# Moving the pieces of weight joining inside a chunk, the order of early loads, and the place of four conversions, in a fused attention and two-layer feed-forward kernel

## The chip, the cores and the metric

One core of one Trainium2 chip runs the whole kernel. The metric is device time in microseconds (us), from three runs of the kernel, of which the median stands here. One more execution was taken under the hardware profiler; every duration below comes from that one.

## What is computed

The reference, cut down to what matters:

```python
# attention: q, k, v are (4, 8, 576, 64), float32
scores = scale * q @ k.T + bias[h]           # ALiBi bias, causal window of 128
attn = softmax(scores); out = attn @ v       # -> x, (2304, 512)
# first layer: w_in (512, 2048), w_out (2048, 512)
h = x @ w_in
P = a0 + a1*h + a2*h*h + a3*h*h*h
Q = 1 + |b0|*|h| + |b1|*h*h
x = (P / (Q + 1e-6)) @ w_out
# second layer, other weights of the same sizes
h = x @ w_in
out = where(h > 0, h, exp(min(h, 0)) - 1) @ w_out
```

The weights of both layers arrive as float64. [...]

## The kernel before, in words

**Attention.** 16 units (a batch entry and a pair of heads each), software pipelined: iteration `t` of the loop at line 684 runs the table `STEPS` (line 18), in which each step names how many iterations it lies ahead or behind. q, k and v of a unit come by transfers that SyncE (SP) issues, in program order, from one queue. `load(u + 3, "qk")` is called at step `zT` (line 643), `load(u + 2, "v")` at step `Y` (line 648). There are two v buffers, so v of unit u+2 can only be fetched after step `Y` of unit u. `load_some(2)` (line 686) fetches two float64 weight tiles of the first layer in each of the iterations 0 to 11.

**Conversion.** A weight tile of the first layer takes five instructions: `conv_scale` (ScalarE, line 130), `conv_shift` (VectorE, line 138), `conv_or` (VectorE, line 148), `conv_hi` (the rounded part, line 156 or 158) and `conv_lo` (the rest, line 162). `PLAN` (line 32) says how many tiles are converted beside which attention unit: 24 of the 32 there. Then `CONV_AFTER` (line 33) calls `conv_step` six times in the last iterations, and `conv_step` is called in the first layer's first block (line 1267). `conv_step` puts its VectorE parts into a list, `put_off`, which `go_on` works off one by one.

**First layer.** Tokens go in five blocks (512, 512, 512, 256, 512 columns), a block in 16 chunks of 128 hidden units; chunk number `s` runs over all 80 (line 1263). TensorE alternates `gemm1(s)` (12 matmuls, line 287) and `gemm2_T(s - 3)` (12 matmuls, line 725); each product is three passes, over high and low parts of both factors. Between them lies `rational` (line 302): ScalarE makes the square, |h|, two affine terms (lines 311 to 314), later a logarithm and an exponential (lines 325, 326), which give 1/Q; VectorE makes the rest (lines 319 to 340), and from chunk 5 on GpSimd (POOL) makes the low part of the result (line 337). `rational(s)` finishes chunk s-1 and begins chunk s on the same queues.

`rational` takes callables that are put between its instructions. In blocks 1 and 2 they **join** second-layer weights: per chunk two half tiles n and n+1, each `join_scale` (ScalarE, line 130, reads a fetched half, writes a buffer: `space_u` for even n, `space_w1` for odd n), `join_shift` (VectorE, line 138), `join_words` (VectorE, line 800), then a copy out to DRAM (line 810) and the fetch of half n+3 (line 776). There are 26 such chunks, 13 in each of the two blocks.

At a block's end `split_x` (line 256) splits the next block's input into high parts (ScalarE, line 268) and low parts (VectorE, line 269), four of each, into the buffers that `gemm1` has just read. `conv_until` in `gemm1` and `gemm2_T` would force a conversion that is late.

**Second layer.** Its order comes from a planner (`in_order`, line 1153). Neither the planner nor its costs are touched.

The scale in the middle of a joined chunk is placed by this call (lines 1280 to 1283):

```python
rational(
    s, after=lambda: join_scale(nj + 1),
    beside=(first_join, lambda: join_shift(nj + 1), lambda: join_end(nj + 1)),
)
```

Of the kernel before, what the change touches and what calls it, by code (L numbers as in the profile page):

```python
# [28 lines left out]
)  # L29


PLAN = (0, 0, 0) + (2,) * 12 + (0,) * 4
CONV_AFTER = ((15, "E8"), (15, "R1"), (14, "V1"), (15, "T01"), (15, "T11"), (15, "V1"))
AHEAD = {
    (14, "T00"): 1, (14, "T10"): 1, (14, "T11"): 2, (14, "V0"): 1, (14, "V1"): 2, (14, "Y"): 1,
# [9 lines left out]
def kernel(  # L45
# [125 lines left out]
    def go_on():  # L171
        if put_off:
            put_off.pop(0)()
# [79 lines left out]
    def bank(n, shape, name):  # L253
        return psum.tile(shape, F32, tag=f"b{n}", name=name)

    def split_x(j, rounds="AAAA"):
        t0, n = BL[j]
        if j == 0:
            for tag in ("qa", "qb", "ta", "bi"):
                cut(tag, SIZE[tag], F32R)  # L260
        parts = {"hi": [], "lo": []}
        for c in range(KD):
            src = xT[:, c, t0:t0 + n]
            hi, lo = row1(f"hi{c}", j * KF), row1(f"lo{c}", j * KF)
            if rounds[c] == "D":
                nc.vector.tensor_copy(hi, src)
            else:
                nc.scalar.activation(out=hi, in_=src, func=AF.Copy)  # L268
            nc.vector.tensor_tensor(out=lo, in0=src, in1=hi.bitcast(F32), op=ALU.subtract)  # L269
            parts["hi"].append(hi)  # L270
            parts["lo"].append(lo)
        return parts
# [26 lines left out]
        for c in range(4):  # L299
            yield from gemm1(c, c, x1[0], 4 + c)  # L300

    def rational(c, old=True, beside=3 * (lambda: None,), after=lambda: None):


        old = old and c - 1 in q_t
        new = c in h_t
        if new:
            h = h_t.pop(c)
            h2, ee, qq, rr = [row1(nm, c) for nm in ("h2", f"ee{c % 2}", f"qq{c % 2}", f"rr{c % 2}")]
            qa = bank(6, [P, width(c)], "qa") if c > 3 else qq  # L310
            nc.scalar.activation(out=h2, in_=h, func=AF.Square)  # L311
            nc.scalar.activation(out=qa, in_=h, func=AF.Abs, scale=b_abs[:, 0:1])  # L312
            nc.scalar.activation(out=ee, in_=h, func=AF.Identity, scale=a_sb[:, 1:2], bias=a_sb[:, 0:1])  # L313
            nc.scalar.activation(out=h, in_=h, func=AF.Identity, scale=a_sb[:, 3:4], bias=a_sb[:, 2:3])  # L314
        if old:
            qq0, ee0, rr0 = q_t.pop(c - 1)
            hi, low = row1(f"ghi{c % 3}", c - 1), row1(f"glo{c % 3}", c - 1)
            g_t[c - 1] = (hi, low)
            nc.vector.tensor_tensor(out=hi, in0=ee0, in1=rr0, op=ALU.mult)  # L319
        beside[0]()  # L320
        if new:
            nc.vector.scalar_tensor_tensor(  # L322
                out=qq, in0=h2, scalar=b_abs[:, 1:2], in1=qa, op0=ALU.mult, op1=ALU.add
            )
            nc.scalar.activation(out=rr, in_=qq, func=AF.Ln, bias=c_q)  # L325
            nc.scalar.activation(out=rr, in_=rr, func=AF.Exp, scale=-1.0)
            q_t[c] = (qq, ee, rr)
        after()
        beside[1]()
        if old:  # L330
            nc.vector.scalar_tensor_tensor(
                out=qq0, in0=qq0, scalar=EPSC, in1=hi.bitcast(F32), op0=ALU.add, op1=ALU.mult
            )
        beside[2]()
        if old:
            nc.vector.tensor_tensor(out=ee0, in0=ee0, in1=qq0, op=ALU.subtract)  # L336
            (nc.gpsimd if c > 4 else nc.vector).tensor_tensor(out=low, in0=ee0, in1=rr0, op=ALU.mult)  # L337
        if new:
            nc.vector.tensor_tensor(out=h, in0=h2, in1=h, op=ALU.mult)  # L339
            nc.vector.tensor_tensor(out=ee, in0=ee, in1=h, op=ALU.add)  # L340


    def attention():
        with ExitStack() as es:
# [284 lines left out]
            def run(step, u):  # L629
                if step[0] in CONV:  # L630
                    if 0 <= u < len(PLAN) and int(step[1]) < PLAN[u]:
                        n = sum(PLAN[:u]) + int(step[1])
                        eng = ENG.get(step)
                        CONV[step[0]](order[n], *([eng] if eng else []))
                        if step[0] == "s":
                            to_conv.pop(0)
                elif 0 <= u < NU:
                    RUN[step](u)
                    if u == 0 and step == "kT":
                        warm(1)  # L640
                    if step == "zT":
                        if u + 3 < NU:
                            load(u + 3, "qk")
                        elif u == NU - 1:
                            load_some(4)
                    elif step == "Y":
                        if u + 2 < NU:
                            load(u + 2, "v")
                        else:
                            load_some(2)  # L650

# [30 lines left out]

            first = -max(late for _, late in STEPS)
            for t in range(first, NU + 2):
                if 0 <= t < 12:
                    load_some(2)
                if t == NU - 1:
                    x1[0] = split_x(0, "DADA")
# [22 lines left out]
    def experts():  # L711
# [519 lines left out]
        def prepare(s):  # L1231
            f = s - LAST
            if f == 3:
                load_wi(0)
            if f == 14:
                load_wi(1)
                for e in raw_ones(0):
                    load_raw(0, e)

            def copies():  # L1240
                for fn in AT_ACT.get(f, []):
                    fn()

            def next_one():
                if f >= 3 and AT_DVE:
                    AT_DVE.pop(0)()
            rational(s, beside=(lambda: None, next_one, next_one), after=copies)

        def joins(s):

# [12 lines left out]
        for s in range(NCH):  # L1263
            o = s - SK
            j, f = divmod(s, KF)
            if j == 0 and f % 2 and f > 2:
                conv_step(to_conv, later=True)
            if s >= 4:
                run_all(gemm1(s, f, x1[j], (4, 5, 7)[(s - 4) % 3]))
            if f == KF - 1 and j + 1 < NB:  # L1270
                x1[j + 1] = split_x(j + 1)
            if o >= 0:
                gemm2_T(o)
            if joins(s) == 2:

                def first_join():
                    join_shift(nj)
                    join_end(nj)

                rational(  # L1280
                    s, after=lambda: join_scale(nj + 1),
                    beside=(first_join, lambda: join_shift(nj + 1), lambda: join_end(nj + 1)),
                )
            elif joins(s):
                rational(s, beside=(lambda: None, lambda: join_shift(nj), lambda: join_end(nj)))
            elif s >= LAST:
                prepare(s)
            else:
                rational(s, beside=(go_on, go_on, go_on))
            nj += joins(s)  # L1290
            if s == KF - 2:
                for n in range(3):
                    load_half(n)
            if joins(s + 1):
                join_scale(nj)
# [41 lines left out]
```

## Time and profile before

| what | value |
|---|---|
| median of 3 runs (lowest, highest) | 948.56 us (947.55, 950.12) |
| the profiled execution | 951.53 us, its span 949.7 us |
| mean granted TensorE clock, share of full speed | 0.992 |
| TensorE busy with matmuls | 920.9 us (97%) |
| VectorE busy | 787.3 us (83%) |
| ScalarE busy | 710.8 us (75%) |
| GpSimd busy | 175.9 us (19%) |

The profiled execution took 2.97 us longer than the median of the three runs; its span, first to last instruction, is 1.83 us shorter than its own time. A sum worked out on the span is a difference, and is taken off 951.53 us and off 948.56 us alike.

A row of the timeline reads: start in us from the span's beginning, duration, engine, line of the kernel, operation, what it writes and reads, and in brackets how long the engine sat idle before it and what ended that. A row's duration reaches from its start to its end; on one engine the next row may start before that end.

### The profile page before, as it was taken

What the parts mean: (1) busy time and instruction counts of PE and PEld (TensorE: products, weight loads), DVE (VectorE), ACT (ScalarE), POOL (GpSimd) and SP (SyncE); (2) the same over time, 40 slices, a digit from 0 to 9 for tenths busy, and PEclk for the clock granted to TensorE, in tenths of its full rate; (3) what the DMA queues carried; (4) which work ended last, traced back from release to release, by engine and by line L of the source; (5) the groups of instructions that cost most, each with busy time, mean ns of one, the idle gap of its engine ahead of it and who ended that gap; (6) DMA issues with size and microseconds to landing.
All of it is one profiled execution on the core that took longest, in us unless ns stands there. A gap on an engine that the chain in (4) does not pass through costs nothing.

```text
span 949.7 us, 15573 instructions
## 1 busy us (share of the span) xinstructions
PE 920.9 (97%) x5110; PEld 776.2 (82%) x5110; DVE 787.3 (83%) x1773; ACT 710.8 (75%) x1510; POOL 175.9 (19%) x238
## 2 busy tenths in 40 slices
PE   8999999999999899979999999999999999999998
PEld 5777777888877687759988888898989898989897
DVE  7699999998788877887889898999967778787653
ACT  6899997887767777778888777676867566766553
POOL 4466661122122211222222220000000000000000
PEclk9899999999999999999999999999999999999999
DMA  9899842000333323230010033445334332442201
GB/s 172 212 247 247 222 148 69 1 12 23 112 121 106 94 90 126 99 109 1 1 35 1 1 101 110 133 153 203 111 128 139 102 99 71 167 140 90 78 0 67
DMA packets 112560, 98.27 MB, mean 103 GB/s; under 512 B 62816, under 2 KB 86368, under 8 KB 112480
## 3 DMA queue, kind: packets, MB, share of 16 engines
q1 hardware_dynamic: 109936, 96.57, 34.5%
q10 hardware_dynamic: 2544, 0.72, 0.4%
q8 instruction: 40, 0.66, 0.3%
q14 instruction: 40, 0.33, 0.1%
HBM read 79.96 MB, written 17.30 MB: 102 GB/s over the span
## 4 chain that ended last, share of the span: by engine, by line
PE 70%; DVE 19%; DMA 4%; ACT 3%; issue 2%; DVEq 0%; SPq 0%; ACTq 0%
PE acc L951 21%; PE m L935 18%; PE acc L725 14%; PE h L287 13%; DVE space_g L319 2%; DVE xT L340 2%; DVE xT L336 2%; DVE h L339 2%; DVE pr_wi L518 1%; DMA joined_wi<-space_u 1%; DVE pr_wo L518 1%; DMA v<-in_v_dram 1%; DVE cvt L148 1%; DMA joined_wo<-space_u 1%; PE s_ps L492 1%
## 5 line engine op out<-in xcount | busy, mean ns | idle before, releaser
L725 PE MATMUL acc<-space_g,w_wo 128*128 128x512 f32 (+1 forms) x960 | 217.2, 372 | 9.1 <-POOL space_g L337 8.3
L725 PEld LDWEIGHTS acc<-space_g,w_wo 128*128 128x128 f32 x960 | 168.5, 190 | 46.0 <-POOL space_g L337 15.1
L337 POOL TENSOR_TENSOR space_g<-xT,space_r 128x512 fp32r<-128x512 f32 (+1 forms) x76 | 89.4, 1176 | 329.3 <-DVE xT L336 239.3
L951 PE MATMUL acc<-op_wo,space_g 128*128 128x512 f32 x432 | 108.2, 393 | 0.0
L287 PE MATMUL h<-space_qa,w_wi 128*128 128x512 f32 (+1 forms) x320 | 91.9, 371 | 4.1 <-ACT space_qa L268 3.4
L951 PEld LDWEIGHTS acc<-op_wo,space_g 128*128 128x128 f32 x432 | 80.5, 188 | 14.7
L311 ACT ACTIVATE space_u<-h 128x512 f32<-128x512 f32 (+1 forms) x80 | 44.3, 554 | 62.9 <-DVE h L339 43.3
L997 ACT ACTIVATE space_u<-space_r 128x384 f32<-128x384 f32 x48 | 25.1, 523 | 75.3 <-DVE space_r L991 74.4
L287 PE MATMUL h<-space_qb,w_wi 128*128 128x512 f32 (+1 forms) x240 | 76.1, 371 | 3.8 <-DVE space_qb L269 3.8
L935 PE MATMUL m<-xo_wi,op_wi 128*128 128x384 f32 x336 | 77.3, 337 | 0.0
L935 PE MATMUL m<-xo_wo,op_wi 128*128 128x384 f32 x336 | 76.4, 335 | 0.0
L287 PE MATMUL h<-space_ta,w_wi 128*128 128x512 f32 (+1 forms) x240 | 76.1, 372 | 0.0
L287 PEld LDWEIGHTS h<-space_qa,w_wi 128*128 128x128 f32 x320 | 57.5, 189 | 15.0 <-ACT space_qa L268 4.2
L322 DVE SCALAR_TENSOR_TENSOR xT<-space_u,b_abs,qa 128x512 f32<-128x512 f32 (+1 forms) x76 | 52.2, 687 | 16.6 <-ACT qa L312 16.4
L325 ACT ACTIVATE space_r<-xT,c_q 128x512 f32<-128x512 f32 (+1 forms) x80 | 55.1, 689 | 13.7 <-DVE xT L322 13.4
L935 PEld LDWEIGHTS m<-xo_wo,op_wi 128*128 128x128 f32 x336 | 60.9, 188 | 4.1
L935 PEld LDWEIGHTS m<-xo_wi,op_wi 128*128 128x128 f32 x336 | 60.6, 188 | 0.0
L287 PE MATMUL h<-space_bi,w_wi 128*128 128x512 f32 (+1 forms) x160 | 59.6, 372 | 0.0
L319 DVE TENSOR_TENSOR space_g<-xT,space_r 128x512 fp32r<-128x512 f32 (+1 forms) x80 | 51.4, 643 | 9.5 <-PE h L287 0.5
L313 ACT ACTIVATE xT<-h,a_sb 128x512 f32<-128x512 f32 (+1 forms) x80 | 59.3, 741 | 0.0
L1001 ACT ACTIVATE space_u<-space_u,c_m 128x384 f32<-128x384 f32 x96 | 57.5, 611 | 1.6
L314 ACT ACTIVATE h<-h,a_sb 128x512 f32<-128x512 f32 (+1 forms) x80 | 57.4, 717 | 0.0
(187 smaller groups left out, 2120.2 us busy)
## 6 DMA issues: line engine op xcount, KB each, us to landing
space_qa<-joined_wo SPq DMA_DIRECT2D x43, 256.0 KB, 2.6
raw_wo<-in_moe_w_out_dram SPq DMA_DIRECT2D x20, 512.0 KB, 4.9
raw_wi<-in_moe_w_in_dram SPq DMA_DIRECT2D x16, 512.0 KB, 4.3
half<-in_moe_w_in_dram SPq DMA_DIRECT2D x32, 256.0 KB, 2.7
two_wo<-joined_wi SPq DMA_DIRECT2D x32, 256.0 KB, 2.9
s<-sums SPq DMA_DIRECT2D x32, 256.0 KB, 2.7
half<-in_moe_w_out_dram SPq DMA_DIRECT2D x22, 256.0 KB, 2.8
v<-in_v_dram SPq DMA_DIRECT2D x32, 128.0 KB, 3.5
```

The source lines that it names most:

```text
L287: nc.tensor.matmul(h, lhsT=WT["wi", f][:, SEL[wp], kk * P:(kk + 1) * P], rhs=x[xp][kk], start=(kk == 0 and n == 0), stop=(kk == KD - 1 and ...
L311: nc.scalar.activation(out=h2, in_=h, func=AF.Square)
L313: nc.scalar.activation(out=ee, in_=h, func=AF.Identity, scale=a_sb[:, 1:2], bias=a_sb[:, 0:1])
L314: nc.scalar.activation(out=h, in_=h, func=AF.Identity, scale=a_sb[:, 3:4], bias=a_sb[:, 2:3])
L319: nc.vector.tensor_tensor(out=hi, in0=ee0, in1=rr0, op=ALU.mult)
L322: nc.vector.scalar_tensor_tensor(out=qq, in0=h2, scalar=b_abs[:, 1:2], in1=qa, op0=ALU.mult, op1=ALU.add)
L325: nc.scalar.activation(out=rr, in_=qq, func=AF.Ln, bias=c_q)
L337: (nc.gpsimd if c > 4 else nc.vector).tensor_tensor(out=low, in0=ee0, in1=rr0, op=ALU.mult)
L725: nc.tensor.matmul(acc_t[d], lhsT=WT["wo", f][:, SEL[wp], d * P:(d + 1) * P], rhs=gt[SEL[xp]], start=(f == 0 and n == 0), stop=(f == KF - ...
L935: nc.tensor.matmul(out, lhsT=w[:, SEL[wp], c0:c0 + P], rhs=XO[q // NP2, nm, k][:, SEL[xp]], start=(k == 0 and n == 0), stop=(k == 1 and n ...
L951: nc.tensor.matmul(acc_t[T, t], lhsT=gt[SEL[xp]][:, t * P:(t + 1) * P], rhs=w[:, SEL[wp]], start=(first and n == 0), stop=(last and n == 2),)
L1001: nc.scalar.activation(out=e, in_=e, func=AF.Identity, bias=c_m)
```

## The change

Six edits:

- `rational` has four places for callables in place of three, and no `after`: ahead of the old chunk's `hi` product (line 319), ahead of `qq` (line 322), behind the exponential, and ahead of the subtraction (line 336).
- In a joined chunk the second half's scale now stands on ScalarE's queue ahead of the logarithm, and on VectorE the first half's shift ahead of the `hi` product.
- `PLAN` converts 20 tiles beside attention, none beside units 3 and 4; the weight tiles are fetched in iterations 2 to 13; the first layer's first block calls `conv_step` from chunk 1 on.
- For units 3 to 5, q and k of unit u+3 are fetched behind v, in the others as before.
- `split_x` at a block's end makes the third and fourth low part on GpSimd.
- Chunks with one join, and those without, pass the same callables to the new places.

```diff
-PLAN = (0, 0, 0) + (2,) * 12 + (0,) * 4
+PLAN = (0,) * 5 + (2,) * 10 + (0,) * 4
...
-    def split_x(j, rounds="AAAA"):
+    def split_x(j, rounds="AAAA", lows="DDDD"):
...
-            nc.vector.tensor_tensor(out=lo, in0=src, in1=hi.bitcast(F32), op=ALU.subtract)
+            (nc.gpsimd if lows[c] == "G" else nc.vector).tensor_tensor(
+                out=lo, in0=src, in1=hi.bitcast(F32), op=ALU.subtract
+            )
...
-    def rational(c, old=True, beside=3 * (lambda: None,), after=lambda: None):
+    def rational(c, old=True, beside=4 * (lambda: None,)):
...
+        beside[0]()
         if old:
...
             nc.vector.tensor_tensor(out=hi, in0=ee0, in1=rr0, op=ALU.mult)
-        beside[0]()
+        beside[1]()
         if new:
...
-        after()
-        beside[1]()
+        beside[2]()
         if old:
...
-        beside[2]()
+        beside[3]()
         if old:
...
                         if u + 3 < NU:
-                            load(u + 3, "qk")
+                            put_off.append(lambda: load(u + 3, "qk"))
+                            if u < 3 or u > 5:
+                                go_on()
...
                             load(u + 2, "v")
+                            go_on()
...
-                if 0 <= t < 12:
+                if 2 <= t < 14:
                     load_some(2)
...
-            if j == 0 and f % 2 and f > 2:
+            if j == 0 and f % 2:
                 conv_step(to_conv, later=True)
...
-                x1[j + 1] = split_x(j + 1)
+                x1[j + 1] = split_x(j + 1, lows="DDGG")
...
-                def first_join():
-                    join_shift(nj)
-                    join_end(nj)
-
-                rational(
-                    s, after=lambda: join_scale(nj + 1),
-                    beside=(first_join, lambda: join_shift(nj + 1), lambda: join_end(nj + 1)),
-                )
+                def begin():
+                    join_scale(nj + 1)
+                    join_shift(nj)
+
+                rational(s, beside=(
+                    begin, lambda: join_end(nj), lambda: join_shift(nj + 1), lambda: join_end(nj + 1),
+                ))
             elif joins(s):
-                rational(s, beside=(lambda: None, lambda: join_shift(nj), lambda: join_end(nj)))
+                rational(s, beside=(lambda: join_shift(nj), lambda: join_end(nj)) + 2 * (lambda: None,))
...
-                rational(s, beside=(go_on, go_on, go_on))
+                rational(s, beside=(go_on, lambda: None, go_on, go_on))
```

In the rows below the changed kernel's line numbers are higher by 2 to 5 (its L322 is L319 of before, L325 is L322, L333 is L331, L338 is L336, L341 is L339, L342 is L340, L805 is L800).

**A joined chunk on ScalarE**, before: `half_3065` is half n, `half_3111` half n+1, `half_3121` the next chunk's first.

```order
L130 ACTIVATE space_u<-half_3065 128x256
L311 ACTIVATE space_u<-h 128x512
L312 ACTIVATE qa<-h,b_abs 128x512
L313 ACTIVATE xT<-h,a_sb 128x512
L314 ACTIVATE h<-h,a_sb 128x512
L325 ACTIVATE space_r_76<-xT,c_q 128x512
L326 ACTIVATE space_r_76<-space_r_76 128x512
L130 ACTIVATE space_w_2421<-half_3111 128x256
L130 ACTIVATE space_u<-half_3121 128x256
```

Now:

```order
L130 ACTIVATE space_u<-half_3065 128x256
L313 ACTIVATE space_u<-h 128x512
L314 ACTIVATE qa<-h,b_abs 128x512
L315 ACTIVATE xT<-h,a_sb 128x512
L316 ACTIVATE h<-h,a_sb 128x512
L130 ACTIVATE space_w_2399<-half_3112 128x256
L328 ACTIVATE space_r_76<-xT,c_q 128x512
L329 ACTIVATE space_r_76<-space_r_76 128x512
L130 ACTIVATE space_u<-half_3121 128x256
```

The scale of the second half went from behind the exponential (L326) to ahead of the logarithm (L325 of before, L328 now); the next chunk's first scale stays at the end.

**The same chunk on VectorE**, before:

```order
L340 TENSOR_TENSOR xT<-xT,h 128x512
L319 TENSOR_TENSOR space_g<-xT,space_r_75 128x512
L138 TENSOR_SCALAR half_3065<-half_3065 128x256
L800 SCALAR_TENSOR_TENSOR space_u<-space_u,half_3065 128x256
L322 SCALAR_TENSOR_TENSOR xT<-space_u,b_abs,qa 128x512
L138 TENSOR_SCALAR half_3111<-half_3111 128x256
L331 SCALAR_TENSOR_TENSOR xT<-xT,space_g 128x512
L800 SCALAR_TENSOR_TENSOR space_w_2421<-space_w_2421,half_3111 128x256
L336 TENSOR_TENSOR xT<-xT 128x512
L339 TENSOR_TENSOR h<-space_u,h 128x512
L340 TENSOR_TENSOR xT<-xT,h 128x512
```

Now:

```order
L342 TENSOR_TENSOR xT<-xT,h 128x512
L138 TENSOR_SCALAR half_3065<-half_3065 128x256
L322 TENSOR_TENSOR space_g<-xT,space_r_75 128x512
L805 SCALAR_TENSOR_TENSOR space_u<-space_u,half_3065 128x256
L325 SCALAR_TENSOR_TENSOR xT<-space_u,b_abs,qa 128x512
L138 TENSOR_SCALAR half_3112<-half_3112 128x256
L333 SCALAR_TENSOR_TENSOR xT<-xT,space_g 128x512
L805 SCALAR_TENSOR_TENSOR space_w_2399<-space_w_2399,half_3112 128x256
L338 TENSOR_TENSOR xT<-xT 128x512
L341 TENSOR_TENSOR h<-space_u,h 128x512
L342 TENSOR_TENSOR xT<-xT,h 128x512
```

The first shift moved ahead of the `hi` product, between two rows of which the second reads what the first writes; the first OR went with the product; the second shift and OR keep their places.

**SyncE in the first iterations**, before (`v_88` is the buffer of v for unit 0, refilled here for unit 2; `qk_wi`, `qk_tails` are q and k of a later unit, `raw` a float64 weight tile):

```order
L374 DMA qk_wi_301<-in_k_dram 128x4x64 x2
L378 DMA qk_tails_wo_92<-in_k_dram 64x2x64
L704 DMA a_sb<-in_moe_a_dram 128x4
L705 DMA b_raw<-in_moe_b_dram 128x2
L112 DMA raw_wi_341<-in_moe_w_in_dram 128x4x256
L117 DMA raw_wo_343<-in_moe_w_out_dram 128x1024
L374 DMA qk_wi_403<-in_q_dram 128x4x64 x2
L378 DMA qk_tails_wo_92<-in_q_dram 64x2x64
L374 DMA qk_wi_403<-in_k_dram 128x4x64 x2
L378 DMA qk_tails_wo_92<-in_k_dram 64x2x64
L374 DMA v_88<-in_v_dram 128x4x64 x2
L378 DMA v_88<-in_v_dram 64x2x64
```

Now:

```order
L376 DMA qk_wi_297<-in_q_dram 128x4x64 x2
L380 DMA qk_tails_wo_92<-in_q_dram 64x2x64
L376 DMA qk_wi_297<-in_k_dram 128x4x64 x2
L380 DMA qk_tails_wo_92<-in_k_dram 64x2x64
L709 DMA a_sb<-in_moe_a_dram 128x4
L710 DMA b_raw<-in_moe_b_dram 128x2
L376 DMA v_88<-in_v_dram 128x4x64 x2
L380 DMA v_88<-in_v_dram 64x2x64
L376 DMA qk_wi_440<-in_q_dram 128x4x64 x2
L380 DMA qk_tails_wo_92<-in_q_dram 64x2x64
```

The fetch of v for unit 2 stands behind one q and k pair and the coefficients; the raw tiles and the next unit's q and k stood ahead of it, and stand behind it now.

**VectorE where attention ends and chunk 0 is finished**, before (`cvt` and `raw` are a tile under conversion):

```order
L156 CAST w_wo_2376<-cvt_2319 128x512
L162 TENSOR_TENSOR w_wo_2376<-cvt_2319,w_wo_2376 128x512
L461 COPY xT<-ty 128x64
L461 COPY xT<-x 128x512
L319 TENSOR_TENSOR space_g<-xT,space_r_75 128x512
L331 SCALAR_TENSOR_TENSOR xT<-xT,space_g 128x512
L336 TENSOR_TENSOR xT<-xT 128x512
L337 TENSOR_TENSOR space_g<-xT,space_r_75 128x512
```

Now:

```order
L138 TENSOR_SCALAR raw_wi_1998<-raw_wi_1998 128x512
L148 SCALAR_TENSOR_TENSOR cvt_2317<-cvt_2317,raw_wi_1998 128x512
L162 TENSOR_TENSOR w_wo_2350<-cvt_2291,w_wo_2350 128x512
L463 COPY xT<-ty 128x64
L463 COPY xT<-x 128x512
L138 TENSOR_SCALAR raw_wo_2000<-raw_wo_2000 128x512
L322 TENSOR_TENSOR space_g<-xT,space_r_75 128x512
L148 SCALAR_TENSOR_TENSOR cvt_2352<-cvt_2352,raw_wo_2000 128x512
L333 SCALAR_TENSOR_TENSOR xT<-xT,space_g 128x512
L162 TENSOR_TENSOR w_wi_2402<-cvt_2317,w_wi_2402 128x512
L338 TENSOR_TENSOR xT<-xT 128x512
L339 TENSOR_TENSOR space_g<-xT,space_r_75 128x512
```

A shift and an OR stand ahead of the copies to `xT`, and a shift, an OR and a `conv_lo` (L162) between the steps that lead to the low part of chunk 0 (L337 of before, L339 now).

## Rows read from the trace of the kernel before

**Rows 1.** Windows by stage: stretch, length, busy (x count) per engine, PEclk, DMA, GB/s

```profile
160.00:227.50 67.50, 67.50 (x298) 55.87 (x299) 62.73 (x99) 55.94 (x92) 12.99 (x10) 1.00 0.04 12
227.50:332.20 104.70, 97.20 (x410) 77.00 (x410) 84.84 (x159) 77.30 (x137) 21.92 (x17) 0.98 0.32 98
332.20:432.00 99.80, 91.86 (x398) 73.45 (x397) 80.86 (x155) 74.19 (x134) 20.59 (x16) 0.98 0.31 101
```

**Rows 2.** Chain of waits in order of time, first layer: start, us, what

```profile
227.72 2.72 PE h L287 x12
...
307.32 1.73 DMA joined_wi<-space_u
...
332.33 2.72 PE h L287 x12
```

**Rows 3.** Timeline of VectorE, one joined chunk in block 1

```profile
304.35 0.69 DVE L339 TENSOR_TENSOR h<-space_u,h 128x512 f32<-128x512 f32 x1
305.08 0.69 DVE L340 TENSOR_TENSOR xT<-xT,h 128x512 f32<-128x512 f32 x1
305.87 0.69 DVE L319 TENSOR_TENSOR space_g<-xT,space_r 128x512 fp32r<-128x512 f32 x1
306.48 0.29 DVE L138 TENSOR_SCALAR half<-half 128x256 int32<-128x256 int32 x1
306.87 0.43 DVE L800 SCALAR_TENSOR_TENSOR space_u<-space_u,half 128x256 int32<-128x256 int32 x1
307.21 0.74 DVE L322 SCALAR_TENSOR_TENSOR xT<-space_u,b_abs,qa 128x512 f32<-128x512 f32 x1
...
308.07 0.69 DVE L331 SCALAR_TENSOR_TENSOR xT<-xT,space_g 128x512 f32<-128x512 f32 x1
309.73 0.42 DVE L800 SCALAR_TENSOR_TENSOR space_w<-space_w,half 128x256 int32<-128x256 int32 x1 [0.97 <-ACT space_w L130]
...
310.67 0.69 DVE L339 TENSOR_TENSOR h<-space_u,h 128x512 f32<-128x512 f32 x1
```

**Rows 4.** Timeline of ScalarE, the same chunk

```profile
305.13 0.60 ACT L311 ACTIVATE space_u<-h 128x512 f32<-128x512 f32 x1 [1.43 <-DVE h L339]
...
306.86 0.76 ACT L314 ACTIVATE h<-h,a_sb 128x512 f32<-128x512 f32 x1
...
309.28 0.41 ACT L130 ACTIVATE space_w<-half 128x256 f32<-128x256 f32 x1
```

**Rows 5.** Timeline of TensorE, early attention

```profile
24.38 0.40 PE L596 MATMUL ty<-pT,v 128*64 128x64 f32 x8
...
40.27 2.10 PE L585 MATMUL x<-pT,v 128*64 128x128 f32 x12 [0.91 <-DMA v<-in_v_dram]
...
45.11 0.64 PE L596 MATMUL ty<-pT,v 128*64 128x64 f32 x8
...
47.18 0.93 PE L492 MATMUL s_ps<-space_qb 64*128 64x128 f32 x8
...
54.83 0.93 PE L492 MATMUL s_ps<-space_qa 64*128 64x128 f32 x8
```

**Rows 6.** Timeline of SyncE's queue: the fetch of v for unit 2

```profile
35.97 1.98 SPq L374 DMA_DIRECT2D v<-in_v_dram  x2
```

**Rows 7.** Timeline around chunk 0: TensorE and VectorE

```profile
159.85 2.58 PE L725 MATMUL acc<-space_g,w_wo 128*128 128x512 f32 x10 [0.78 <-DVE space_g L337]
...
174.97 0.42 DVE L138 TENSOR_SCALAR raw_wi<-raw_wi 128x512 int32<-128x512 int32 x1
```

**Rows 8.** Timeline of GpSimd and VectorE, low parts at a block's end

```profile
432.36 1.29 POOL L337 TENSOR_TENSOR space_g<-xT,space_r 128x512 fp32r<-128x512 f32 x1 [2.58 <-DVE xT L336]
...
433.12 0.82 DVE L319 TENSOR_TENSOR space_g<-xT,space_r 128x256 fp32r<-128x256 f32 x1
...
466.37 0.43 DVE L319 TENSOR_TENSOR space_g<-xT,space_r 128x256 fp32r<-128x256 f32 x1
```

**Rows 9.** DMA issues: KB each, us from issue to landing

```profile
joined_wi<-space_w SPq DMA_DIRECT2D x16, 128.0 KB, 1.8
```

More of the change, by code (lines that the diff above doesn't have):

```diff
@@ L1242, in copies @@
                     fn()
+                next_one()
             def next_one():
@@ L1246, in next_one @@
                     AT_DVE.pop(0)()
-            rational(s, beside=(lambda: None, next_one, next_one), after=copies)
+            rational(s, beside=(lambda: None, lambda: None, copies, next_one))
         def joins(s):
```

## The prediction

> **What bounds the kernel now.** I read first the busy time of each engine by stage. In the first layer's block 0 (160 to 227.5 us) TensorE works through all of its 67.50 us, at a granted clock of 1.00 [rows 1]. In blocks 1 and 2 it is idle for 104.70 - 97.20 = 7.5 us and 99.80 - 91.86 = 7.9 us, the clock stands at 0.98, and no other engine is full: VectorE has 84.84 of 104.70 us [rows 1]. A stage in which nobody is full is paced by a loop of waits. The chain of waits shows TensorE's own pace, 2.72 us for 12 matmuls, so 5.44 us for a chunk; from the first matmul of block 1 to the first one 17 such steps later 332.33 - 227.72 = 104.61 us went by, where 17 x 5.44 = 92.5 would do [rows 2]. So 12.1 us are lost there.
>
> VectorE's timeline then shows who paces. In a joined chunk the step at line 339 comes at 304.35 and again at 310.67: 6.32 us, not 5.44 [rows 3]. The 0.88 us too many lie where the second OR (line 800, 309.73) sat idle for 0.97 us until ScalarE's scale had ended; that scale started at 309.28, behind the logarithm and the exponential [rows 3, 4]. ScalarE in turn had waited 1.43 us for line 339 before its square [rows 4]. This closes the loop: line 339, square, affine terms, logarithm, exponential, scale, OR, subtraction, line 339. 13 chunks per block x 0.88 = 11.4 us, nearly the 12.1.
>
> Last I read TensorE in early attention, where it waits for v by DMA [rows 5], and the place where chunk 0 is finished [rows 7].
>
> **Part 1, the joined chunks.** The change takes the logarithm and the exponential out of the loop, since the second scale goes ahead of them. Both new loops, by start spacing of the rows:
>
> - Through ScalarE: line 339 to the square 305.13 - 304.35 = 0.78; square to the last affine term 306.86 - 305.13 = 1.73, that term 0.76, the scale 0.41; from OR to the next line 339 310.67 - 309.73 = 0.94. Sum 4.62 us [rows 3, 4].
> - Through VectorE alone: lines 339 to 340 0.73, line 340 0.61 (as the product at line 319 to its follower), shift 0.29, product 0.61, OR 0.34, line 322 and the second shift 0.86, line 331 0.61 (taken as the product), OR to line 339 0.94. Sum 4.99 us [rows 3].
>
> Both lie under 5.44, so TensorE paces the chunk. ScalarE's two scales, square and four other activations keep their durations. The gain: 12.1 us in block 1, and as many in block 2, whose idle time and clock are alike [rows 1]: 24.2 us. I leave 0.6 us of it at the block boundaries: **-23.6 us**. The upper bound is 24.6 (12.1 and, with block 2's larger idle time, 12.5). For the lower I take four hand-overs of the new order to cost what the product's cost before: it started 305.87 - 305.08 = 0.79 us behind line 340, where 0.61 would do, so 0.18 each, 0.72 in all, a chunk of 5.71: 26 x 0.27 = 7 us less, or 17 to 18.
>
> The chunks with one join and those without pass the same instructions in nearly the same order; their joins stand on engines with room (VectorE 84.84 of 104.70) and I put them at nothing.
>
> **Part 2, v ahead of q and k.** TensorE's last v product of unit 0 is at 24.38, of unit 2 at 45.11; between, it waits 0.91 us for v [rows 5]. Two iterations take 45.11 - 24.38 = 20.73 us. Undisturbed, one takes 54.83 - 47.18 = 7.65 us [rows 5], two 15.3. v of unit 2 was issued only at 35.97 [rows 6], since the raw tiles and the next q and k stood ahead of it on SyncE's queue. In the new order these stand behind it. v can go out when unit 0 has read its buffer, at about 25 us, some 10 us earlier, and lands before it is needed at about 39. So 20.73 becomes 15.3: **-5.4 us**. Lower bound 3: the raw tiles come later and with them the conversions, and q and k of unit 5 go behind v. At worst only the slow stretch behind the wait goes (40.27 to 47.18 is 6.9 us, which holds about half of the 5.4). Upper bound 7: the two iterations gain 2.7 each, and I let a third beside them, whose raw tiles go as well, gain half as much. What SyncE issues later, q and k, are needed three iterations on, so 20 us and more are left.
>
> **Part 3, the end of attention.** Four tiles are no longer converted there, so block 0 begins with five conversion steps queued on VectorE ahead of chunk 0's low part: two shifts at 0.42 [rows 7] and two ORs and a low part at 0.69 (the two-input rows of 512 [rows 3]), 2.9 us, less 0.08 each by which neighbours overlap, so 2.4. TensorE already waited 0.78 us for VectorE at that place [rows 7], with no cover left: **+2.4 us**. Bounds 0 (if TensorE arrives later by as much, with attention's own VectorE work lighter) and 3. Behind such a pause the granted clock may fall for a while: blocks 1 and 2 show 0.98 against 1.00 [rows 1], worth 0.02 x 104.7 = 2.1 us in a block. I count half of one: **+1.0**, bounds 0 and 2.1.
>
> **Part 4, four more tiles in block 0.** Each takes a shift, an OR and a low part on VectorE, 0.42 + 0.69 + 0.69, so 7.2 us in all, less overlaps some 6. VectorE is busy 62.73 of 67.50 us by durations over 99 rows; neighbours overlap by 0.08, 7.9 us, so that 12.7 are free [rows 1]. TensorE covers them: **0**. Were the cover gone, the steps would delay chunks by up to 5.4 us.
>
> **Part 5, low parts on GpSimd at four boundaries.** GpSimd takes 1.29 us for such a product [rows 8], two take 2.6; VectorE's four took 4 x 0.61 = 2.4 and now takes two. TensorE starts with the first tiles, so I put it at **0**.
>
> But the two engines may not run beside each other freely. VectorE's product of 128x256 took 0.82 us while GpSimd ran from 432.36 to 433.65, and 0.43 us alone [rows 8]. If VectorE must sit out both GpSimd products in place of doing two of its own, each boundary costs 2.58 - 1.22 = 1.36 us more, four 5.4 us. The Trainium skill ("SBUF — State Buffer", section "SBUF: two separate sides") says that VectorE instructions with two SBUF inputs and GpSimd share a pair of ports that is held exclusively for a whole instruction. The 0.82 against 0.43 agrees with it; by this rule the sum would be -20.2 in place of -25.6.
>
> **The sum.** -23.6 - 5.4 + 2.4 + 1.0 = -25.6 us. The profiled execution took 951.53 us, which gives 925.9; it lay 2.97 us above the median 948.56, so the median to expect is **923.0 us**. A measurement tells about 0.3% (2.8 us) from no change.
>
> **The rivals.**
>
> - *Forecast, 0.72.* 917 to 931, from the bounds of the parts.
> - *GpSimd holds VectorE up at the boundaries, 0.08.* 923.0 + 5.4 = 928.4. For it rows 8; against it, that VectorE is not the last to arrive at every boundary.
> - *Another loop closes halfway, 0.07.* The chunk stops at 5.88 (VectorE's sum is within 0.45 of the limit already): 26 x 0.44 = 11.4 us stay, 934.4. For it: the margin is small. Against it: the low bound above needs four added hand-overs for 5.71.
> - *The scale isn't released, 0.04.* The chain of waits puts the copy out to DRAM of the first half (307.32, 1.73 us) ahead of the scale [rows 2]. If the scale really waited for it, the loop would be: line 339 to the first OR's end 0.73 + 0.61 + 0.29 + 0.61 + 0.43 = 2.7, copy 1.7, scale 0.41, OR to line 339 0.94, with two hand-overs of 0.18 about 6.1 us. Then 26 x 0.22 = 5.7 us are gained and 923.0 + 23.6 - 5.7 = 941 comes out. Against it: the scale writes another buffer than that copy reads, and it starts 0.2 us after that copy's end, just when the exponential is through.
> - *Slower: the scale waits for its own buffer, 0.08.* The scale now stands ahead of the logarithm on ScalarE, in order. It writes the buffer that the same half of the chunk before is copied out from. From that OR's end to the scale a paced chunk leaves 5.44 - 0.45 (scale to OR) - 0.43 (OR) = 4.6 us; the copy lands in 1.8 us [rows 9]. Beyond a landing of 4.6 the logarithm waits with the scale, where formerly only the scale did, and the chunk becomes landing + 0.88. At a landing of 5.5 the gain is gone, at 6.0 a chunk takes 6.88 and 26 x 1.44 = 37 us are lost in place of 24: about 960. DMA is busy a third of the stage [rows 1], so I give it little; 0.03 of the 0.08 lie between, within 0.3% of no change.
> - *Faster than 917, 0.01.*
>
> **How the numbers follow.** The likeliest case gives 923.0. The range must leave out 2 in 10 at most: 915.5 (below the forecast's case, with the upper bounds of parts 1 and 2 and the lower of part 3 nearly together) to 935.5 takes in the forecast, the GpSimd case and the halfway loop, 0.87 before the edges. Faster: 0.72 + 0.08 + 0.07 + 0.04 + 0.01 = 0.92; within 0.3%: 0.03; slower: 0.05.
>
> **What would show it.** Right: joined chunks repeat every 5.44 us, VectorE's second OR has no idle time before it that ScalarE ends, blocks 1 and 2 show TensorE idle for under 1 us each and a clock near 1.00; the wait for v before unit 2's product is gone and two iterations take about 15 us; TensorE waits about 3 us for chunk 0's low part. Wrong: the scale (line 130) in idle time that a DMA ended; a spacing between 5.5 and 6.3; VectorE rows at a boundary stretched beside GpSimd; a wait for q and k in units 6 to 8; block 0 with idle time of TensorE.

## The result, and the profile after

| | kernel before | changed kernel |
|---|---|---|
| median (lowest, highest) | 949.18 us (947.55, 950.12) | 925.15 us (924.16, 926.17) |
| the profiled execution, its span | 951.53, 949.7 us | 924.2, 922.4 us |
| mean granted clock | 0.992 | 1.000 |

The ratio is 0.9749, 95% interval 0.9728 to 0.9770: 24.0 us faster, where 923.0 us were forecast. The time came out within 2.2 us; three of the terms behind it did not come out so well, and their misses partly cancelled.

The windows by stage of the changed kernel, blocks 0, 1 and 2 (length, busy time of TensorE, its weight load, VectorE, ScalarE and GpSimd with counts, granted clock, DMA share, GB/s), answer to [rows 1]:

```profile
160.00:225.00 65.00, 65.00 (x289) 53.81 (x288) 62.54 (x99) 54.89 (x92) 15.33 (x12) 1.00 0.02 5
225.00:312.00 87.00, 87.00 (x386) 72.03 (x385) 80.60 (x151) 73.07 (x131) 23.97 (x19) 1.00 0.41 124
312.00:399.50 87.50, 87.50 (x391) 72.57 (x390) 80.88 (x153) 72.96 (x132) 22.99 (x19) 1.00 0.37 115
```

TensorE is never idle in blocks 1 and 2 now, and the clock is full. The chain of waits in order of time (start, us, what) says the same; it answers to [rows 2]:

```profile
224.83 2.72 PE h L289 x12
...
317.31 2.72 PE h L289 x12
```

Between these two pieces lie 92.48 us, the 17 x 5.44 of the prediction, in place of 104.61. The same stretch of block 2, up to its last group of TensorE's `acc` rows (408.54 us now, 435.99 before), gained 12.4 more. A joined chunk (a scale, a shift and an OR build float32 words from the two 32-bit halves of float64 words), VectorE's timeline, answers to [rows 3]:

```profile
302.13 0.69 DVE L341 TENSOR_TENSOR h<-space_u,h 128x512 f32<-128x512 f32 x1
302.85 0.69 DVE L342 TENSOR_TENSOR xT<-xT,h 128x512 f32<-128x512 f32 x1
303.45 0.38 DVE L138 TENSOR_SCALAR half<-half 128x256 int32<-128x256 int32 x1
303.75 0.68 DVE L322 TENSOR_TENSOR space_g<-xT,space_r 128x512 fp32r<-128x512 f32 x1
304.35 0.41 DVE L805 SCALAR_TENSOR_TENSOR space_u<-space_u,half 128x256 int32<-128x256 int32 x1
304.93 0.75 DVE L325 SCALAR_TENSOR_TENSOR xT<-space_u,b_abs,qa 128x512 f32<-128x512 f32 x1 [0.17 <-ACT qa L314]
...
306.62 0.42 DVE L805 SCALAR_TENSOR_TENSOR space_w<-space_w,half 128x256 int32<-128x256 int32 x1
...
307.56 0.69 DVE L341 TENSOR_TENSOR h<-space_u,h 128x512 f32<-128x512 f32 x1
```

Line 341 repeats after 5.43 us instead of 6.32. The second OR (306.62) shows no idle time for the scale any more, and VectorE waits a little, 0.17 us, for ScalarE's |h| (`qa`). ScalarE in turn waits for TensorE:

```profile
303.75 0.60 ACT L313 ACTIVATE space_u<-h 128x512 f32<-128x512 f32 x1 [1.00 <-PE h L289]
...
306.14 0.45 ACT L130 ACTIVATE space_w<-half 128x256 f32<-128x256 f32 x1
```

The scale has no idle time before it: no transfer holds it. So TensorE paces here, in the second half of a block. In the first half VectorE is late from the block boundary, catches up, and repeats line 341 faster still:

```profile
232.32 0.69 DVE L341 TENSOR_TENSOR h<-space_u,h 128x512 f32<-128x512 f32 x1
...
237.27 0.68 DVE L341 TENSOR_TENSOR h<-space_u,h 128x512 f32<-128x512 f32 x1
```

These 4.95 us are VectorE's own loop, which the prediction's sum puts at 4.99.

At the end of attention (TensorE's timeline) three waits stand where [rows 7] has one of 0.78 us:

```profile
145.86 1.63 PE L587 MATMUL x<-pT,v 128*64 128x128 f32 x25 [1.12 <-ACT pT L461]
...
153.93 0.70 PE L730 MATMUL acc<-space_g,w_wo 128*128 128x512 f32 x2 [0.39 <-DVE space_g L322]
156.98 2.57 PE L730 MATMUL acc<-space_g,w_wo 128*128 128x512 f32 x10 [2.34 <-DVE space_g L339]
```

The last v products of units 0 and 2 (TensorE's timeline) answer to [rows 5]:

```profile
24.61 0.40 PE L598 MATMUL ty<-pT,v 128*64 128x64 f32 x8
...
39.88 0.40 PE L598 MATMUL ty<-pT,v 128*64 128x64 f32 x8
```

By TensorE's last v products the gain of the profiled execution divides so: unit 0 to unit 2 15.27 us in place of 20.73 (-5.5), unit 2 to unit 14 -1.2, unit 14 to chunk 0's low part 16.21 in place of 12.70 (+3.5), blocks 1 and 2 -12.1 and -12.4. With 0.2 lost ahead of unit 0 this is 27.5, and the span is 27.3 us shorter. Behind block 2, where the chunks with one join lie, the execution takes 513.9 us now and took 513.7.

### The profile page after: what moved, and what is told of

It is laid out like the page before. It is cut to its first block, busy times and chain, and to the rows that moved or that the text cites. A ratio compares the mean times of both kernels' runs of the same rounds, so it can differ in the third digit from the quotient of the medians.

```text
span 922.4 us, 15561 instructions
## 1 busy us (share of the span) xinstructions
PE 907.6 (98%) x5110; PEld 772.2 (84%) x5110; DVE 786.0 (85%) x1761; ACT 710.3 (77%) x1514; POOL 184.5 (20%) x246
## 4 chain that ended last, share of the span: by engine, by line
PE 84%; DVE 11%; ACT 3%; issue 1%; DMA 0%; POOL 0%; ACTq 0%; DVEq 0%; POOLq 0%
PE acc L956 21%; PE acc L730 21%; PE h L289 20%; PE m L940 19%; DVE cvt L148 1%; DVE pr_wi L520 1%; DVE pr_wo L520 1%; PE s_ps L494 1%; PE ps_pT L568 1%; DVE w_wi L162 1%; ACT pr_wo L535 1%; PE x L587 1%; ACT pT L461 1%; DMA qk_tails_wo<-in_k_dram 0%; PE ps_qk L438 0%
## 5 line engine op out<-in xcount | busy, mean ns | idle before, releaser
L730 PE MATMUL acc<-space_g,w_wo 128*128 128x512 f32 (+1 forms) x960 | 210.7, 368 | 2.7 <-DVE space_g L339 2.3
L339 POOL TENSOR_TENSOR space_g<-xT,space_r 128x512 fp32r<-128x512 f32 (+1 forms) x76 | 89.7, 1180 | 295.1 <-DVE xT L338 200.1
L325 DVE SCALAR_TENSOR_TENSOR xT<-space_u,b_abs,qa 128x512 f32<-128x512 f32 (+1 forms) x76 | 52.2, 687 | 20.1 <-ACT qa L314 19.9
L322 DVE TENSOR_TENSOR space_g<-xT,space_r 128x512 fp32r<-128x512 f32 (+1 forms) x80 | 55.0, 687 | 5.3
L328 ACT ACTIVATE space_r<-xT,c_q 128x512 f32<-128x512 f32 (+1 forms) x80 | 55.3, 691 | 5.5 <-DVE xT L325 5.3
```

What stands on the lines that cost most here:

```text
L325: nc.vector.scalar_tensor_tensor(out=qq, in0=h2, scalar=b_abs[:, 1:2], in1=qa, op0=ALU.mult, op1=ALU.add)
L730: nc.tensor.matmul(acc_t[d], lhsT=WT["wo", f][:, SEL[wp], d * P:(d + 1) * P], rhs=gt[SEL[xp]], start=(f == 0 and n == 0), stop=(f == KF - ...
```

## Experiments

Each kernel ran beside the kernel before on one chip; a ratio is that of the two.

**The scale alone, in the kernel before.**

```diff
 def first_join():
+    join_scale(nj + 1)
     join_shift(nj)
     join_end(nj)
...
 rational(
-    s, after=lambda: join_scale(nj + 1),
-    beside=(first_join, lambda: join_shift(nj + 1), lambda: join_end(nj + 1)),
+    s, beside=(first_join, lambda: join_shift(nj + 1), lambda: join_end(nj + 1)),
```

> The kernel before, with nothing changed but the second half's scale, which goes ahead of the logarithm. Loop theory: it alone takes 24 us off, chunks at 5.44, and TensorE's waits at the block boundaries (3.8 and 3.4 us in all before) vanish too, since they were the same loop's lateness. Rival (the boundary waits come from VectorE's four low parts there): 3 to 7 us of waits stay, so 17 to 21 us off.

922.97 us (922.25 to 923.35), ratio 0.9725 [0.9704, 0.9745]: 25.5 us off the 948.44 of the kernel before beside it. The one moved call gives all the gain, and more than the whole change does. The waits at the block boundaries vanished though nothing was edited there: windows by stage, blocks 1 and 2 of this kernel, show TensorE without a pause.

```profile
225.00:312.00 87.00, 87.00 (x385) 72.05 (x384) 78.99 (x152) 72.99 (x130) 20.75 (x16) 1.00 0.39 118
312.00:399.50 87.50, 87.50 (x393) 72.70 (x392) 79.48 (x154) 73.84 (x131) 20.74 (x16) 1.00 0.36 115
```

**The change without the scale's move.** Its call goes from `begin` to just ahead of `join_shift(nj + 1)`.

> The changed kernel, with the second half's scale behind the exponential again; VectorE's shift stays ahead of the product. Loop theory (ScalarE's queue closes the loop): joined chunks repeat every 6.3 us again, VectorE's second OR idles about 1 us for the scale, the time rises by 23 to 25 us to about 949. Rival (the shift between the dependent products brought the gain): under 5 us slower, chunks at 5.44.

943.81 us, ratio 0.9951 [0.9927, 0.9974]. VectorE's timeline of this kernel:

```profile
284.52 0.69 DVE L342 TENSOR_TENSOR xT<-xT,h 128x512 f32<-128x512 f32 x1
...
288.87 0.43 DVE L805 SCALAR_TENSOR_TENSOR space_w<-space_w,half 128x256 int32<-128x256 int32 x1 [0.97 <-ACT space_w L130]
...
289.81 0.69 DVE L341 TENSOR_TENSOR h<-space_u,h 128x512 f32<-128x512 f32 x1
290.54 0.69 DVE L342 TENSOR_TENSOR xT<-xT,h 128x512 f32<-128x512 f32 x1
...
292.37 0.74 DVE L325 SCALAR_TENSOR_TENSOR xT<-space_u,b_abs,qa 128x512 f32<-128x512 f32 x1
```

The 0.97 us of waiting for the scale are back, but line 342 repeats after 6.02 us, not 6.32. The loop is not quite the one foreseen. In the kernel before, the logarithm waits for VectorE's line 322 (L325 in the rows above), and not for ScalarE's affine terms; ScalarE's timeline of the kernel before:

```profile
307.99 0.72 ACT L325 ACTIVATE space_r<-xT,c_q 128x512 f32<-128x512 f32 x1 [0.36 <-DVE xT L322]
```

So this loop runs from line 339 over VectorE's next rows, shift and product among them, to line 322. That took 307.21 - 304.35 = 2.86 us [rows 3] and takes 292.37 - 289.81 = 2.56 us here. The shift's place is worth these 0.30 us a chunk as long as the loop through the exponential paces, by estimate 7.8 us over 26 chunks. The expectation, 949 us, had left it at nothing.

**The change without the shift's move.** `join_shift(nj)` goes from `begin` back behind the product, ahead of `join_end(nj)`.

> The changed kernel, with the first half's shift behind the product again; the scale stays ahead of the logarithm. Loop theory: VectorE's loop grows by the 0.18 us that the product waits, to about 5.2 us, still under 5.44, so no change (925, within 1 us). Rival (the shift is needed as well): chunks of 5.5 us or more, 2 us slower or more.

925.79 us, ratio 0.9752 [0.9730, 0.9774]: no change. Beside the scale's move the shift's place brings no time, only room: line 341 repeats after 5.29 us through most of a block, and after 4.95 us in the changed kernel where VectorE catches up. With TensorE at 5.44 that is a margin of 0.15 in place of 0.49 us.

**One and two more instructions on VectorE.**

```diff
 def begin():
     join_scale(nj + 1)
     join_shift(nj)
+    for _ in range(1):
+        nc.vector.tensor_scalar(
+            out=half[nj], in0=half[nj], scalar1=0, scalar2=None, op0=ALU.logical_shift_right
+        )
```

The second kernel has `range(2)`.

> The changed kernel, with one more VectorE instruction per joined chunk, a shift by 0 of a whole half, 128x512 (0.42 us, 0.33 by start spacing), behind the first half's shift. By the sum of VectorE's loop, 4.99 + 0.33 = 5.32 us, under 5.44: no change, within 1 us. Rival (the margin is used up, or hand-overs cost more): slower by up to 26 x 0.33 = 9 us.

> The same with two such instructions. By the sum 4.99 + 0.66 = 5.65 to 5.8 us: VectorE's loop paces, chunks 0.2 to 0.4 over 5.44, 5 to 9 us slower. Rival (the loop has more room than the sum says): no change.

927.58 us (ratio 0.9768 [0.9752, 0.9784]) and 940.61 us (0.9913 [0.9898, 0.9928]). VectorE's timeline with one:

```profile
285.59 0.37 DVE L138 TENSOR_SCALAR half<-half 128x256 int32<-128x256 int32 x1
286.06 0.43 DVE L1286 TENSOR_SCALAR half<-half 128x512 int32<-128x512 int32 x1
286.40 0.69 DVE L322 TENSOR_TENSOR space_g<-xT,space_r 128x512 fp32r<-128x512 f32 x1
...
289.74 0.69 DVE L341 TENSOR_TENSOR h<-space_u,h 128x512 f32<-128x512 f32 x1
...
295.23 0.69 DVE L341 TENSOR_TENSOR h<-space_u,h 128x512 f32<-128x512 f32 x1
```

From shift to product it takes 0.81 us here and 0.30 without the extra one, so that one costs 0.51, not 0.33. It reads what the shift has just written, and starts 0.47 us behind it, where the product, which doesn't, starts 0.30 behind. A chunk takes 5.49 us; less 0.51 this is 4.98, the prediction's sum of VectorE's loop (4.99). With two, chunks take 5.95 (line 341 at 286.97 and 292.92), and 26 x (5.95 - 5.44) = 13.3 us explain most of the 15.5 us lost. The sum was right, and so is the margin, 0.45 us; the price I gave one instruction was not, which made both expectations too low. Of the 2.4 us that the first kernel loses between medians, 26 x 0.05 = 1.3 are this pace; its granted clock is 0.998 in three of four runs.

**The low parts at the boundaries on VectorE**, `lows="DDDD"`.

> The changed kernel, with all four low parts at a block's end on VectorE. Prediction: no change (within 1 us), VectorE's rows beside them at 0.7 in place of 1.8 us. Rival (GpSimd holds VectorE up): up to 5 us faster. Other rival (the boundary needs GpSimd): TensorE waits at the boundaries again, up to 7 us slower.

925.60 us, ratio 0.9752 [0.9725, 0.9779]: no change. But VectorE's timeline differs. The changed kernel, behind the joined chunk shown above, with GpSimd's rows:

```profile
309.59 1.78 DVE L269 TENSOR_TENSOR space_ta<-xT,space_qa 128x512 fp32r<-128x512 f32 x1
311.29 1.77 DVE L322 TENSOR_TENSOR space_g<-xT,space_r 128x512 fp32r<-128x512 f32 x1
```

```profile
309.50 1.32 POOL L269 TENSOR_TENSOR space_bi<-xT,space_qb 128x512 fp32r<-128x512 f32 x1 [0.38 <-ACT space_qb L268]
310.78 1.73 POOL L269 TENSOR_TENSOR space_bi<-xT,space_ta 128x512 fp32r<-128x512 f32 x1
```

and with all four on VectorE:

```profile
311.21 0.68 DVE L269 TENSOR_TENSOR space_ta<-xT,space_qa 128x512 fp32r<-128x512 f32 x1
...
313.02 0.68 DVE L322 TENSOR_TENSOR space_g<-xT,space_r 128x512 fp32r<-128x512 f32 x1
```

1.78 against 0.68 us: each VectorE product ends 0.55 us behind GpSimd's. Two products lose 2.2 us, and two are saved at 0.6. TensorE waits for none of it.

**The early loads, taken apart.** Three kernels: q and k ahead of v again in units 3 to 5; the raw tiles in iterations 0 to 11 again (`if 0 <= t < 12`); both.

> The changed kernel, with q and k ahead of v in units 3 to 5 again; raw tiles still from iteration 2. If the raw tiles were what held v back: no change. If q and k were: part of the 5.4 us comes back, with a wait of TensorE for v. By the queue, v of unit 2 is put behind one more q and k group (about 4 us of issue), issued at about 30, landing at 34, before 37.6, when it is needed: no change, within 1 us.

> The changed kernel, with the raw tiles fetched in iterations 0 to 11 again; v stays ahead of q and k. By the queue, v of unit 2 is issued at about 29 to 30, behind one pair of raw tiles: in time, unless the DMA engines, full at this point, make it land later than 37.6. Expected 0 to 2 us slower; with a wait for v, 3 to 5 us slower.

> The changed kernel with both orders of the loads as before. Expected: 5.4 us slower, TensorE waits 0.9 us for v and the granted clock falls to 0.5 for about 5 us behind that wait; two iterations take 20.7 us. Rival (the wait came from other work that is gone, such as the conversions beside units 3 and 4): no wait, no change.

925.01 us (0.9753 [0.9739, 0.9768]), 928.07 (0.9785 [0.9769, 0.9801]) and 928.50 (0.9785 [0.9769, 0.9801]). The order of v and q, k is worth nothing; that the raw tiles come two iterations later is worth 2.9 us between medians, both together 3.4. Part of this is the granted clock, which is full in two of four runs of the changed kernel and in one of four with both undone: of runs with the same mean clock, those with both undone are 1.9 us slower at 1.000 (926.03 against 924.16 and 924.20) and about 2.5 at 0.998. With both undone TensorE waits 2.5 us for v, but unit 0 to unit 2 take 17.32 us, not 20.73. The kernel with the scale alone, whose load order is that of before, took 17.28. With only the raw tiles early, v of unit 2 comes in time, and these two units take 15.47 us; but now TensorE waits for v of unit 5:

```profile
63.20 0.43 PE L587 MATMUL x<-pT,v 128*64 128x128 f32 x2 [0.81 <-DMA v<-in_v_dram]
```

The granted clock from 60 to 70 us is 0.78 to 0.88 there, and unit 0 to unit 5 take 43.25 us. From unit 0 to unit 5 the other profiled executions took 46.29 us (before), 42.38 (scale alone), 42.30 (both undone) and 39.92 (changed).

**Raw tiles later, without taking conversions away.** On top of the scale alone: raw tiles in iterations 1 to 12, and in 2 to 13, with 24 tiles converted from unit 3 on as before.

> The kernel before with the second half's scale ahead of the logarithm (as in the run with that edit alone, 922.97 us), and the raw tiles fetched one iteration later, in 1 to 12; all 24 tiles are still converted beside attention. If early raw tiles take DMA time from v: part of the 2.4 us by which that run reached unit 14 later than the changed kernel comes back, 920.6 to 922.5 us, with 12.7 us from unit 14's last v product to chunk 0's low part as before. Rival (the first conversions now wait for their tiles on ScalarE): no gain, or slower.

> The same with the raw tiles in iterations 2 to 13, as the change has them, and 24 tiles converted beside attention from unit 3 on. The first tile's scale stands in the iteration that fetches it. If it waits there for its transfer (about 5 us and more): ScalarE stands, attention is 2 to 8 us later, 923 to 930 us. Rival (it lands in time): 920.5, the early gain of the change without its price at attention's end.

929.57 us (0.9804 [0.9788, 0.9821]) and 1017.62 us (1.073 [1.0711, 1.0749]). ScalarE's timeline, first the one, then the other:

```profile
32.22 0.69 ACT L130 ACTIVATE cvt<-raw_wi 128x512 f32<-128x512 f32 x1 [4.82 <-DMA raw_wi<-in_moe_w_in_dram]
```

```profile
35.61 0.69 ACT L130 ACTIVATE cvt<-raw_wi 128x512 f32<-128x512 f32 x1 [8.58 <-DMA raw_wi<-in_moe_w_in_dram]
...
68.07 0.67 ACT L130 ACTIVATE cvt<-raw_wi 128x512 f32<-128x512 f32 x1 [5.41 <-DVE w_wo L162]
```

One wait for a tile, with attention's exponentials queued behind it, costs more than the later tiles bring. The second kernel is far slower than the 923 to 930 us expected: a wait of about 5 us for a conversion buffer comes ten times in attention, on ScalarE and then on TensorE, and the granted clock is 0.75 to 0.78 from 40 to 160 us. As far as these two kernels show, the later tiles, the later conversions and the four tiles that move to the first layer belong together: the first is the gain, the others make it possible, and the last has the price at attention's end.

**That price.** No conversion step beside chunk 0:

```diff
-rational(s, beside=(go_on, lambda: None, go_on, go_on))
+rational(s, beside=(go_on, lambda: None, go_on, go_on) if s > 1 else 4 * (lambda: None,))
```

> The changed kernel, with the three conversion steps that stand between chunk 0's products on VectorE moved behind its low part (none are run beside chunk 0). If these make TensorE wait 2.3 us there: the wait falls by 1.6 to 1.9 us, and the time with it. Rival (chunk 0 is late for another reason, or the steps are late next): same wait, or one elsewhere in block 0.

923.80 us (923.34 to 924.15), ratio 0.9741 [0.9727, 0.9756].

```profile
155.49 2.58 PE L730 MATMUL acc<-space_g,w_wo 128*128 128x512 f32 x10 [1.39 <-DVE space_g L339]
```

TensorE's wait for chunk 0's low part fell from 2.34 to 1.39 us and the 0.39 ahead of it went; 0.6 us came back as a wait for the next chunk's low part. That leaves 0.7 us in the waits, less than expected, since the steps are late next, as the rival says. Between medians it is 1.3 us, because the granted clock is full or nearly so (0.999) in all four runs here and only in two of the changed kernel; the changed kernel's two runs at full clock are 0.4 us behind this median.

## Why the prediction came out right, and where it did not

- **Part 1 was right, near its upper bound**: 24.5 us in the trace, 25.5 between medians, against 23.6. TensorE paces now at 5.44. The loop was closed by the scale behind the exponential, as read; its way from line 339 to the logarithm was misread. It went over VectorE's shift, product and line 322, not over ScalarE's affine terms, which were done 0.37 us before the logarithm began (306.86 + 0.76 against 307.99). The sum for the new order was not touched by this. The 0.6 us left for the boundaries were not needed; the waits there had been the same loop's lateness. What the text of part 1 took as one thing is one line of the change: the scale. The shift's move takes no time off beside it.
- **Part 2 was right for the execution it was read from and too large for the kernel.** The trace shows -5.5 where -5.4 was forecast, but the medians 2.9 to 3.4, and runs with the same clock 1.9 to 2.5. The step that failed is the term's size: 20.73 us for two iterations was a bad case of a stretch that took 17.3 in two other executions with the same load order. What made it bad was the granted clock behind the wait, 0.50, the lower of its two levels, up to 46 us:

```profile
40.00:45.00 5.00, 4.73 (x32) 3.80 (x34) 2.67 (x12) 1.99 (x7) 3.32 (x7) 0.50 1.09 293
```

  In the two other executions it stays at 1.00 from 40 to 46 us, though TensorE had waited 0.86 us for v in the one (scale alone) and 1.57 in the other (both undone). The same 16 v products, before and with both undone:

```profile
43.35 1.98 PE L585 MATMUL x<-pT,v 128*64 128x128 f32 x16
```

```profile
41.19 1.09 PE L587 MATMUL x<-pT,v 128*64 128x128 f32 x16
```

  The prediction saw a slow stretch there and took it for a part of every late v. That profiled execution lay 2.4 us above its median, and part of the excess probably lay here: six us at half the clock are 3 us. No other execution of the kernel before was profiled, so it is not settled. If so, taking -25.6 off 951.53 and off the median alike counted it twice. The cause was half right: at unit 2 either move clears the wait, but only the later raw tiles take time off.
- **Part 3 was too small.** +2.4 was forecast (its own rows give 2.9 - 5 x 0.08 = 2.5), +3.5 came. The wait at chunk 0 grew by 1.95 us, 2.34 and 0.39 against 0.78, as foreseen. Not foreseen was the 1.12 us wait of the attention products for ScalarE's copies. ScalarE's timeline of the changed kernel:

```profile
144.64 0.69 ACT L130 ACTIVATE cvt<-raw_wi 128x512 f32<-128x512 f32 x1 [0.97 <-DVE w_wo L162]
145.24 1.06 ACT L461 ACTIVATE pT<-ps_pT 128x512 f32<-128x512 f32 x2
```

  All six steps of `CONV_AFTER` now start a new tile, and a scale waits for a conversion buffer that VectorE still reads, with the copies queued behind. I had costed the steps that moved past chunk 0 on VectorE, and not asked what stands behind a scale on ScalarE.
- **The clock, +1.0 as half of 2.1, came out by luck.** The four runs of the changed kernel are 924.16, 924.20, 926.11 and 926.17 us, with mean clocks of 1.000, 1.000, 0.998 and 0.998: about 2 us in two of four, and the median lies between. The windows behind the pause at chunk 0 show both cases, the changed kernel's profiled execution and that of the kernel with `lows="DDDD"`:

```profile
156.00:166.00 10.00, 9.02 (x40) 7.47 (x41) 9.83 (x17) 8.22 (x13) 0.00 (x0) 1.00 0.00 0
```

```profile
156.00:166.00 10.00, 9.02 (x33) 7.27 (x34) 9.83 (x17) 8.22 (x13) 0.00 (x0) 0.83 0.00 0
```

  The ten matmuls behind the pause take 2.57 us in the one and 4.15 in the other, behind the same 2.34 us of waiting. Of the nine traces with this pause, seven show 0.66 or 0.83 in this stretch and two 1.00, so half may be too low.
- **Parts 4 and 5 cost nothing, as forecast**: block 0 has no idle time of TensorE, and the low parts change the time neither way. The rival on GpSimd had its mechanism right: two VectorE products lose 2.2 us and two are saved at 0.6 us each, so VectorE loses 1.0 us a boundary, where 1.36 was the price. But nothing waits there. By the sentence of the Trainium skill ("SBUF — State Buffer", "SBUF: two separate sides"), that the port pair is held for a whole instruction, VectorE's product waits out GpSimd's; the 0.55 us by which it ends later agrees.
- **The other rivals**: no loop closed halfway, the margin is the 0.45 us of the sum (one extra instruction of 0.51 uses it up); the moved scale waits for no copy, neither the other buffer's nor its own (the first half's scale, which did not move, waits once, 0.33 us, for its own).

Between medians the sum is then -25.5 (scale), -2.4 (loads, unit 0 to unit 5 with both undone against the changed kernel), +3.5 (attention's end), these two from the traces, and about +1 (clock, in half of the runs): -23.4, measured -24.0. Against the forecast's terms the join was 1.9 better, the loads 3.0 worse and attention's end 1.1 worse. Together this is the 2.2 us by which 923.0 was too low. The median of the kernel before, 949.18 over all its runs in place of 948.56, would account for 0.6 more; these 0.6 us stay unexplained, and its medians beside the experiments, 948.25 to 948.88, differ as much.

The fastest kernel measured is the one before with the scale alone: its runs, 922.25 to 923.35 us, lie all below those of the changed kernel. But its VectorE repeats after 5.29 us, 0.15 us under TensorE's pace, so it has the smaller margin. What stays open is whether the later raw tiles can be had without the heavier end of attention; the two kernels that tried it failed at the first conversions.

## What to carry to other kernels

Where no engine is full and one chunk repeats too slowly, follow the chain until it closes, and ask which instruction stands in that loop only by its place in a queue: moving that one alone took off 25.5 us here, the whole change 24.0. An edit inside a loop that no longer paces is worth nothing, so test edits one by one, in both directions; the parts don't add. And a stall read from one execution should be looked for in a second one before its full size enters a sum, above all one with a low granted clock behind it.

## What the runs showed of the hardware

- GpSimd slows down too: its second low part beside VectorE's products took 1.73 us, the first 1.32, where 1.29 was usual [rows 8].
- The same pause of TensorE, 2.34 us, is followed by a stretch at a lower granted clock in some executions and not in others, seven of nine traces here; after the 1.39 us pause of the last experiment none of four runs was 2 us longer. In early attention the clock was 0.50 behind a wait for v of 0.91 us in one execution, and 1.00 behind waits of 1.42 and 0.15 us in another.
- A VectorE instruction in place on what its predecessor wrote started 0.47 us behind it, one that did not read it 0.30 behind; the extra instruction cost 0.51 us in place of the 0.33 expected. That the reading is the reason is an inference; the product's 0.79 us behind line 340, whose result it reads, against 0.61 [rows 3] fits it.
